# One decode step of attention and a feed-forward layer on one core: a weight transfer cut at row 126, two transfers joined, and one head's softmax put ahead of a loop

## The chip, the cores and the metric

The kernel runs on one NeuronCore of a Trainium2 chip. The core has a matrix engine (TensorE, PE in the profile; PEld is its loading of weights), a vector engine (VectorE, DVE), an activation engine (ScalarE, ACT), GpSimd (POOL) and SyncE (SP), which issues nearly all DMA transfers here. 16 DMA engines move the bytes. TensorE writes only into PSUM; all else lies in SBUF, 128 rows (partitions) wide.

The metric is the device time of one execution in microseconds (us), as the median of several runs. A profiled execution has a time of its own, and a span: from its first to its last profiled instruction.

## The reference

One token of width 512 goes through a modulated attention block with a cache of 32768 positions (32 query heads in 8 groups, a group's four heads share K and V of width 128) and then a modulated feed-forward block.

```python
mod = (_silu(c) @ w_mod).reshape(c.shape[0], 6, 1, -1)
sa, ca, ga, sb, cb, gb = ...
h = _layernorm(x) * (1 + ca) + sa
q = (h @ wq), k and v: the caches, each repeated for 4 query heads
p = _softmax(q @ k^T * 128 ** -0.5)
x = x + ga * ((p @ v) @ wo)
h = _layernorm(x) * (1 + cb) + sb
x = x + gb * (maximum(h @ w1, 0) @ w2)
```

K and V are 8 x 32768 x 128 in bf16, 64 MB each; with wq, wo (4 MB each), w_mod (3 MB), w1 and w2 (1.75 MB each) about 149 MB are read once.

## The kernel before

**The stream.** All large inputs come in one fixed order through one queue (SP): w_mod, wq, then for each group of heads ("head" below, 0 to 7) two tiles of K and two of V of 4 MB each, the K of head h + 1 alternating with the V of head h. The last head's second V tile comes as two halves, then wo in four parts (`WOP`, L47: heads 0 to 3, heads 4 and 5, head 6, head 7), w1 in two pieces, w2 in six (`W2P`, L51). The list is `stream` (L139 to L144); `need` (L147) issues it up to the entry that is asked for, through `load` (L96) and `stream_dma` (L131). Tiles lie in a ring of five slots of 4 MB; a transfer can't start before the slot is free. wo's four parts share one slot and w1 and w2 another. Each transfer takes one of eight completion semaphores in turn, and SP waits, before it issues a transfer, until the earlier one with that semaphore has landed.

**One head.** `turn_k` (L398) transposes a quarter of a K tile in place on VectorE (128 x 2048 as f32), four times per 4 MB tile; `scores` (L412) multiplies each of these with the queries on TensorE, 8 matmuls of 128 x 512; after a tile's 32 matmuls `bank_max` (L427) copies the scores to SBUF and takes their maximum. `softmax` (L433) is a generator, whose steps the schedule places one by one with `next(soft)`: m_p, the maximum of each row (L437); mT, its transpose on TensorE (L440); Mrow and Mexp on VectorE (L443, L448); Mb on TensorE, then nbias and the exponential on ScalarE (L454 to L459); PT, the transposed probabilities, and Lexp on VectorE (L465, L468); L_ps, the sums, on TensorE (L471); and Linv, their reciprocals, on VectorE (L474). `pv` (L477) multiplies PT with a V tile: 32 matmuls, in a hardware loop of 8 turns except in the last tiles, where they are written out. `blocks` (L509) picks Y from the result on VectorE, `o_cols` (L520) turns it on TensorE, `normalise` (L528) divides by the sums, `spread` (L544) shapes a part of wo's heads for `project` (L555), which multiplies them with that part of wo.

**The order.** On TensorE and VectorE the order is the one written in the schedule (L599 on): within each engine, instructions start in that order. In iteration g (L611) head h = g + 1 gets its scores, head g its `pv`, and head g - 1 its `blocks` to `normalise`. The first K tile's four transposes and scores come before the first `pv` loop of g, the second tile's between the first and second loop. Head h's softmax begins at the end of iteration g: its first step before the second `pv` loop of g, the second right behind it, and the rest between the scores of iteration g + 1:

```python
            bank_max(h, 1)
            soft = softmax(h)
            next(soft)
            if g < LOOPED:
                pv(g, (2, 3))
                next(soft)
                continue
```

**The tail.** After the scores of head 7 come `pv` for head 6's second and head 7's V tiles, `project(0)` to `project(3)`, the second layernorm (L691 on), w1 (L714), the relu (L725), w2 (L735), the last two VectorE operations (L740, L742) and the 1 KB output. `keep_clock` (L592) multiplies something whose result is not used, in places where TensorE would else wait. `join_rows` (L576) gathers what the first two parts of wo gave.

Of the kernel before, what the change touches and what calls it, by code (L numbers as in the profile page):

```python
# [17 lines left out]
def kernel(  # L18
# [15 lines left out]
    P = 128  # L34
    _, _, D = A_x.shape
    _, Hkv, Sk, Dh = A_k_cache.shape
    Hq = A_wq.shape[1] // Dh
    REP = Hq // Hkv
# [8 lines left out]
    WOP = [(0, Hkv // 2), (Hkv // 2, Hkv // 4), (Hkv - 2, 1), (Hkv - 1, 1)]  # L47
    WOROWS = 2
    LAST = Hkv - 1
    LOOPED = Hkv - 2  # L50
    W2P = [(0, 4), (4, 7), (7, 10), (10, 12), (12, 13), (13, 14)]  # L51
    W1P = [(0, KT - 1), (KT - 1, KT)]
    assert Dh == 128 and REP == 4 and D == 512 and FT == W2P[-1][1] and NTILE == 4
    scale = float(Dh) ** -0.5
    eps = 1e-5
# [5 lines left out]
    vv = A_v_cache[0].rearrange("g (p j) d -> g p j d", p=P)  # L61
    wm_v = w_mod.rearrange("(p kt) n -> p kt n", p=P)
    wq_v = A_wq.rearrange("(p kt) n -> p kt n", p=P)
    def wo_v(i):
        g0, n = WOP[i]
        return A_wo[g0 * REP * Dh:(g0 + n) * REP * Dh, :].rearrange("(p r) d -> p r d", p=P)

    w1_v = B_w1.rearrange("(p kt) f -> p kt f", p=P)
    w2_v = B_w2.rearrange("(p f) d -> p f d", p=P)

# [15 lines left out]
    loaded, last_loop = {}, []  # L86
# [3 lines left out]
    def piece(name, at, n):  # L90

        if name not in pieces:
            pieces[name] = ring.tile([P, 2 * TK * Dh], BF16, tag="slot", name=name)
        return pieces[name][:, at:at + n]

    def load(key):  # L96
        kind = key[0]
        if kind == "wm":
            t = ring.tile([P, KT, 6 * D], BF16, tag="slot", name="wm_sb")
            src = wm_v  # L100
        elif kind == "wq":
            t = ring.tile([P, KT, Hq * Dh], BF16, tag="slot", name="wq_sb")
            src = wq_v
        elif kind in "kv":
            g, steps = key[1], key[2]
            src = (kv if kind == "k" else vv)[g, :, TK * steps[0]:TK * (steps[-1] + 1), :]
            name = "Ksb" if kind == "k" else "Vsb"
            if len(steps) == 2:
                t = ring.tile([P, TK * len(steps), Dh], BF16, tag="slot", name=name)
            else:  # L110
                t = piece(name, TK * Dh * (steps[0] % 2), TK * Dh).rearrange("p (j d) -> p j d", d=Dh)
        elif kind == "wo":
            g0, n = WOP[key[1]]
            t = piece("wo_sb", g0 * REP * D, n * REP * D).rearrange("p (r d) -> p r d", d=D)
            src = wo_v(key[1])
        elif kind == "w1":
            k0, k1 = W1P[key[1]]
            t = piece("w12_sb", k0 * Dff, (k1 - k0) * Dff).rearrange("p (kt f) -> p kt f", f=Dff)
            src = w1_v[:, k0:k1]
        else:  # L120
            f0, f1 = W2P[key[1]]
            t = piece("w12_sb", KT * Dff + f0 * D, (f1 - f0) * D).rearrange("p (f d) -> p f d", d=D)
            src = w2_v[:, f0:f1]
        stream_dma(t[:], src)
        if kind in "kv":
            for i, u in enumerate(steps):
                loaded[(kind, g, u)] = t[:, TK * i:TK * (i + 1), :]
        else:
            loaded[key] = t[:]

    def stream_dma(dst, src):  # L131
        i = nc.sync.dma_start(out=dst, in_=src)
        tc.stamp_issue_order_token(i.ins, "sp_stream")
        if last_loop:

            tc.add_manual_dep(i.ins, last_loop[0], mybir.DependencyInfo(
                mybir.DependencyClass.NoSync, mybir.DependencyReason.DATA))

    stream = [("wm",), ("wq",)] + [("k", 0, (2 * G, 2 * G + 1)) for G in range(NG)]  # L139
    for g in range(LAST):  # L140
        for G in range(NG):
            stream += [(kind, gg, (2 * G, 2 * G + 1)) for kind, gg in (("k", g + 1), ("v", g))]
    stream += [("v", LAST, (0, 1)), ("v", LAST, (2,)), ("v", LAST, (3,))] + [("wo", i) for i in range(len(WOP))]
    stream += [("w1", i) for i in range(len(W1P))] + [("w2", i) for i in range(len(W2P))]  # L144
    pos = [0]

    def need(key):  # L147
        while key not in loaded:
            load(stream[pos[0]])
            pos[0] += 1  # L150
        return loaded[key]
# [17 lines left out]
    for hp in range(4):  # L169
        h, par = hp // 2, hp % 2  # L170
        src = AP(ib.tensor, ib.offset + 64 * h + par, [[ib.ap[0][0], P], [0, 4], [2, 32]])
# [68 lines left out]
    def bank(name):  # L240
        return ps_s.tile([P, 512], F32, tag="s", name=name)[:]
# [137 lines left out]
    def build_qbd(g):  # L379
        d_ap = qbd[g % 2][:]  # L380
        d_ps = d_ap.ap[0][0]
        s_ap = qrep_sb[:]
        s_ps = s_ap.ap[0][0]
        for a in range(4):
            o = AP(d_ap.tensor, d_ap.offset + (32 * a) * d_ps + 4 * 7 + 32 * a,
                   [[d_ps, 32], [QW, 4], [1, 4]])
            i = AP(s_ap.tensor, s_ap.offset + (32 * a) * s_ps + REP * g,
                   [[s_ps, 32], [Hq, 4], [1, 4]])
            nc.scalar.copy(out=o, in_=i)  # L389
# [8 lines left out]
    def turn_k(g, u, half):  # L398

        if u == 0 and half == 0:  # L400
            S_tiles[g] = spool.tile([P, NG, 512], F32, tag="S_g", name="S_g")
            m_tiles[g] = spool.tile([P, NG], F32, tag="m2", name="m2")
        Ksb = need(("k", g, u))
        KTt = Ksb[:, 32 * half:32 * half + 32, :].rearrange("p j d -> p (j d)")
        t = nc.vector.transpose(out=KTt.bitcast(F32), in_=KTt.bitcast(F32))  # L405
        KT_tiles[g, u, half] = KTt
        if loop:

            tc.add_manual_dep(t.ins, loop.pop(), mybir.DependencyInfo(
                mybir.DependencyClass.NoSync, mybir.DependencyReason.DATA))  # L410

    def scores(g, u, half):  # L412

        t4 = (2 * u + half) % 4
        if t4 == 0:
            S_ps_tiles[g] = bank("S_ps")
        KTv = KT_tiles.pop((g, u, half)).rearrange("p (jj h i par) -> p jj h i par", jj=32, h=2, i=32, par=2)
        for sl in range(2):
            s = 2 * t4 + sl
            for hp in range(4):  # L420
                h, par = hp // 2, hp % 2
                nc.tensor.matmul(  # L422
                    S_ps_tiles[g], lhsT=qbd[g % 2][:, hp, 4 * (7 - s):4 * (7 - s) + P], rhs=KTv[:, 16 * sl:16 * sl + 16, h, :, par],
                    start=(t4 == 0 and sl == 0 and hp == 0), stop=(t4 == 3 and sl == 1 and hp == 3),
                )
# [77 lines left out]
    def open_o(g):  # L503
        o_tiles[g] = ps_o.tile([16, 4 * Dh], F32, tag="o", name="o_ps")
        nc.vector.memset(o_tiles[g][:], 0.0)  # L505
# [93 lines left out]
    with tc.manual_schedule(engines={mybir.EngineType.PE, mybir.EngineType.DVE}):  # L599
# [7 lines left out]
        soft = softmax(0)  # L607
        for _ in soft:
            pass
        soft = None  # L610
        for g in range(LAST):  # L611
            h = g + 1
            build_qbd(h)
            turn_k(h, 0, 0)
            turn_k(h, 0, 1)
            turn_k(h, 1, 0)
            scores(h, 0, 0)
            if soft:
                next(soft)
            open_o(g)  # L620
            scores(h, 0, 1)
            if soft:
                next(soft)
            if g > 0:
                blocks(g - 1)
            scores(h, 1, 0)
            if g > 0:
                o_cols(g - 1)
            turn_k(h, 1, 1)
            scores(h, 1, 1)  # L630
            if soft:
                next(soft)
            if g > 0:
                normalise(g - 1)
                if g in [sum(w) for w in WOP]:
                    spread(part_of(g - 1))
            if soft:
                next(soft)
            bank_max(h, 0)
            next(soft or iter(()), None)  # L640
            pv(g, (0, 1))
            for u in (2, 3):
                for half in range(2):
                    turn_k(h, u, half)
                    scores(h, u, half)
            bank_max(h, 1)
            soft = softmax(h)
            next(soft)
            if g < LOOPED:
                pv(g, (2, 3))  # L650
                next(soft)
# [3 lines that stand above are left out]
            pv(g, (2,), range(6))  # L655
            next(soft)
            next(soft)
            open_o(LAST)
            pv(g, (2,), range(6, 16))
            pv(g, (3,))  # L660
            next(soft)
            next(soft, None)
            a_rows.append(row_bank("a_ps"))
            blocks(g)
# [44 lines left out]
        NQ = 32 * FT  # L709
        for part, (k0, k1) in enumerate(W1P):  # L710
            w1_sb = need(("w1", part))
# [62 lines left out]
```

## Time and profile before

| | |
|---|---|
| time, median of 3 runs | 355.38 us (355.25 to 355.55) |
| time of the profiled execution | 355.74 us |
| its span | 353.9 us, mean granted TensorE clock 0.947 |
| TensorE busy | 279.8 us (79%) |
| VectorE busy | 203.1 us (57%) |
| ScalarE busy | 25.4 us (7%) |
| share of the 16 DMA engines in SP's queue | 98.4% |
| read from HBM | 149.42 MB, 422 GB/s over the span |
| a 4 MB tile, from issue to landing | about 35 us (median) |

The busy time of an engine is an average over stages with different limits. The issue-to-landing time of a tile is mostly time in the queue, since a 4 MB tile alone takes about 9.7 us at this rate. "Granted clock" is the share of full speed at which TensorE was allowed to run; the profile shows stretches at 1.0 and at 0.5. In lists of instructions the idle time before a group and what ended it stand in square brackets.

### The profile page before, as it was taken

Reading aid. Unit: us, or ns where it says so; the run is one execution under the profiler, and the core shown is the slowest. Engines: PE = TensorE matmul, PEld = TensorE weight load, DVE = VectorE, ACT = ScalarE, POOL = GpSimd, SP = SyncE. Lnnn points to the kernel's source line nnn. Section 1 sums busy time; section 2 is a strip of 40 time slices with the busy share of each in tenths; the row PEclk is TensorE's granted clock in tenths of the full one; section 3 lists DMA queues with packets and bytes.
Section 4 is the critical chain, followed back from the end, with each engine's and each line's share of the span. In section 5 each row is a group of like instructions: output and inputs, shape, how many; then the busy total and the mean of one; then the engine's idle time right before and its main releaser. Section 6 shows DMA issues by size and latency. Waiting matters only on the chain. (4 is left out here: it accounts for less than half of the span.)

```text
span 353.9 us, 4006 instructions
## 1 busy us (share of the span) xinstructions
PE 279.8 (79%) x1311; PEld 112.7 (32%) x1311; DVE 203.1 (57%) x271; ACT 25.4 (7%) x69; POOL 3.9 (1%) x16
## 2 busy tenths in 40 slices
PE   0542781999898979897979796979689687989996
PEld 0221230333343323332323232323234233334444
DVE  6245775882768268462939178553938095734142
ACT  1220003000010001000100001000100010002000
POOL 4000000000000000000000000000000000000000
PEclk9995997799899999998999899999999997999999
DMA  8999999999999999999999999999999999999994
GB/s 309 455 422 445 431 422 441 441 418 424 459 418 422 459 418 424 441 437 426 433 444 417 430 456 419 427 446 426 422 448 430 422 439 441 422 430 424 421 420 177
DMA packets 6852, 149.59 MB, mean 423 GB/s; under 512 B 824, under 2 KB 1080, under 8 KB 1976
## 3 DMA queue, kind: packets, MB, share of 16 engines
q1 hardware_dynamic: 6776, 149.43, 98.4%
q8 instruction: 8, 0.13, 0.1%
q14 instruction: 4, 0.03, 0.0%
q0 software_dynamic: 64, 0.00, 0.0%
HBM read 149.42 MB, written 0.00 MB: 422 GB/s over the span
## 5 line engine op out<-in xcount | busy, mean ns | idle before, releaser
L405 DVE STREAM_TRANSPOSE Ksb<-Ksb 128x2048 f32<-128x2048 f32 x64 | 142.9, 2281 | 63.9 <-DMA Ksb<-in_A_k_cache_dram 63.9
L484 PE MATMUL o_ps<-Vsb,PT_g 128*16 (+1 forms) x512 | 130.0, 395 | 21.5 <-ACT qbd L389 7.2
L422 PE MATMUL S_ps<-Ksb,qbd 128*128 128x512 bf16 x512 | 121.8, 388 | 23.5 <-DVE Ksb L405 21.9
L422 PEld LDWEIGHTS <-qbd 128*128 128x128 bf16 x512 | 49.0, 98 | 87.6 <-issue 31.8
L484 PEld LDWEIGHTS o_ps<-Vsb,PT_g 128*16 x416 | 37.4, 90 | 90.2 <-issue 63.7
L428 DVE TENSOR_SCALAR_CACHE_REDUCE S_g<-S_ps 128x512 f32<-128x512 f32 x16 | 11.0, 690 | 34.4 <-PE S_ps L422 34.4
L389 ACT COPY qbd<-qrep_sb 32x16 bf16<-32x16 bf16 x32 | 6.4, 201 | 138.7 <-PE S_ps L422 137.6
L465 DVE STREAM_TRANSPOSE PT_g<-P_g 128x1024 bf16<-128x1024 bf16 x8 | 9.7, 1218 | 6.6 <-ACT P_g L459 6.6
L484 PEld LDWEIGHTS <-PT_g 128*16 128x16 bf16 x96 | 8.2, 90 | 11.0
L456 ACT ACTIVATE nbias<-Mb_ps 128x1 f32<-128x1 f32 x8 | 1.4, 171 | 136.8 <-PE Mb_ps L454 136.8
L459 ACT ACTIVATE P_g<-S_g,nbias 128x1024 bf16<-128x1024 f32 x8 | 9.2, 1148 | 0.2
L227 PE MATMUL xc_ps<-cx_sel,cx_bd 16*128 16x2 bf16 x4 | 0.3, 172 | 11.1 <-DVE cx_bd L221 11.1
L515 DVE SCALAR_TENSOR_TENSOR Y<-o_ps,smask,Y 16x128 f32<-16x128 f32 x24 | 8.1, 339 | 0.8
L471 PE MATMUL L_ps<-Lexp,ones_f 128*128 128x4 f32 x16 | 3.0, 257 | 4.3 <-DVE Lexp L468 4.3
L597 PE MATMUL spare_ps<-qbd,ident_bf 128*128 128x512 bf16 x19 | 5.6, 380 | 0.0
L440 PE MATMUL mT_ps<-ident_f,m_p 128*1 128x128 f32 x8 | 2.2, 270 | 3.9 <-DVE m_p L437 2.0
L471 PEld LDWEIGHTS L_ps<-Lexp,ones_f 128*128 128x128 f32 x16 | 3.1, 221 | 5.8 <-issue 5.1
L443 DVE TENSOR_REDUCE Mrow<-mT_ps 1x4 f32<-1x128 f32 x8 | 2.1, 257 | 4.6 <-PE mT_ps L440 4.6
L534 DVE TENSOR_TENSOR oT_sb<-acc_ps,Linv 128x4 bf16<-128x4 f32 x8 | 1.2, 150 | 5.7 <-PE acc_ps L521 5.7
L295 PE MATMUL mod_ps<-wm_sb,siluT 128*1 128x512 bf16 x24 | 3.6, 624 | 1.0 <-DVE siluT L289 1.0
L505 DVE MEMSET o_ps<- 16x512 f32 x8 | 3.9, 485 | 0.8
L552 DVE CAST o_sb<-o_ps 128x4 bf16<-128x4 f32 (+2 forms) x4 | 0.7, 167 | 5.7 <-PE o_ps L548 5.7
(115 smaller groups left out, 80.0 us busy)
## 6 DMA issues: line engine op xcount, KB each, us to landing
Ksb<-in_A_k_cache_dram SPq DMA_DIRECT2D x16, 4096.0 KB, 35.6
Vsb<-in_A_v_cache_dram SPq DMA_DIRECT2D x15, 4096.0 KB, 35.2
wq_sb<-in_A_wq_dram SPq DMA_DIRECT2D x1, 4096.0 KB, 19.6
Vsb<-in_A_v_cache_dram SPq DMA_DIRECT2D x2, 2048.0 KB, 31.8
wm_sb<-in_w_mod_dram SPq DMA_DIRECT2D x1, 3072.0 KB, 10.4
wo_sb<-in_A_wo_dram SPq DMA_DIRECT2D x1, 2048.0 KB, 29.1
w_sb<-in_B_w_dram SPq DMA_DIRECT2D x1, 1344.0 KB
wo_sb<-in_A_wo_dram SPq DMA_DIRECT2D x1, 1024.0 KB, 31.1
```

The source lines that it names most:

```text
L295: nc.tensor.matmul(dst[j // 4][32 * (j % 4):32 * (j % 4) + 1, :], lhsT=src_T[:, kt:kt + 1], rhs=w[:, kt, j * 512:(j + 1) * 512], start=(kt ...
L389: nc.scalar.copy(out=o, in_=i)
L405: t = nc.vector.transpose(out=KTt.bitcast(F32), in_=KTt.bitcast(F32))
L422: nc.tensor.matmul(S_ps_tiles[g], lhsT=qbd[g % 2][:, hp, 4 * (7 - s):4 * (7 - s) + P], rhs=KTv[:, 16 * sl:16 * sl + 16, h, :, par], start= ...
L428: nc.vector.tensor_scalar(out=S_tiles[g][:, G, :], in0=S_ps_tiles[g], scalar1=1.0, scalar2=None, op0=ALU.mult, op1=ALU.max, accum_out=m_ti ...
L459: nc.scalar.activation(out=P_g[:], in_=S_g[:].rearrange("p g f -> p (g f)"), func=ACT.Exp, bias=nbias[:], scale=scale, accum_out=l_g[:],)
L465: nc.vector.transpose(out=PT_g[:], in_=P_g[:])
L471: nc.tensor.matmul(L_ps[:], lhsT=ones_f[:], rhs=Lexp[:], start=True, stop=True)
L484: nc.tensor.matmul(o_tiles[g][:], lhsT=PT, rhs=Vx, start=False, stop=False, skip_group_check=True)
L505: nc.vector.memset(o_tiles[g][:], 0.0)
L515: nc.vector.scalar_tensor_tensor(out=Y[:], in0=o[:, s], scalar=smask[:, s:s + 1], in1=Y[:], op0=ALU.mult, op1=ALU.add,)
L597: nc.tensor.matmul(spare[0], lhsT=ident_bf[:], rhs=qbd[0][:, :, 0:P], start=True, stop=True)
```

## The change

Three things, in one diff:

- `load` can cut a transfer by rows. w2's second piece (3 of 14 columns, 384 KB) goes as one transfer of rows 0 to 125 and one of rows 126 and 127, both into the same place as before.
- wo's third and fourth part, 512 KB each, are one transfer of 1 MB. A key of the stream now names a tuple of parts; `project(2)` and `project(3)` use their halves of it.
- In iteration g = 5 the softmax of head 6 takes four more steps (mT; Mrow and Mexp; Mb, nbias and the exponential; PT and Lexp) before the second `pv` loop of head 5, and L_ps right behind it. In iteration g = 6 (`ahead`) the fourth K transpose of head 7's first tile comes next to the other three, Linv next, then the four groups of scores with only `open_o` and `blocks` between them, and then `o_cols` and `normalise` of head 5.

The number of transfers is the same. The arithmetic is the same.

```diff
+    EVEN, EVEN_ROWS = ("w2", 1), 126
...
         elif kind == "wo":
-            g0, n = WOP[key[1]]
-            t = piece("wo_sb", g0 * REP * D, n * REP * D).rearrange("p (r d) -> p r d", d=D)
-            src = wo_v(key[1])
+            parts = key[1]
+            (g0, n), m = WOP[parts[0]], len(parts)
+            t = piece("wo_sb", g0 * REP * D, m * n * REP * D).rearrange("p (g x) -> p g x", g=m)
+            src = A_wo[g0 * REP * Dh:(g0 + m * n) * REP * Dh, :].rearrange("(g p r) d -> p g (r d)", g=m, p=P)
...
-        stream_dma(t[:], src)
+        cuts = [0, EVEN_ROWS, P] if key == EVEN else [0, P]
+        for a, b in zip(cuts, cuts[1:]):
+            stream_dma(t[a:b], src[a:b])
...
+        elif kind == "wo":
+            for m, i in enumerate(parts):
+                loaded[("wo", i)] = t[:, m].rearrange("p (r d) -> p r d", d=D)
...
-    stream += [("v", LAST, (0, 1)), ("v", LAST, (2,)), ("v", LAST, (3,))] + [("wo", i) for i in range(len(WOP))]
+    stream += [("v", LAST, (0, 1)), ("v", LAST, (2,)), ("v", LAST, (3,))] + [("wo", parts) for parts in ((0,), (1,), (2, 3))]
...
         for g in range(LAST):
             h = g + 1
+            ahead = h == LAST
             build_qbd(h)
             turn_k(h, 0, 0)
             turn_k(h, 0, 1)
             turn_k(h, 1, 0)
+            if ahead:
+                turn_k(h, 1, 1)
+                next(soft, None)
+                soft = None
             scores(h, 0, 0)
...
             scores(h, 1, 0)
+            if ahead:
+                scores(h, 1, 1)
             if g > 0:
                 o_cols(g - 1)
-            turn_k(h, 1, 1)
-            scores(h, 1, 1)
+            if not ahead:
+                turn_k(h, 1, 1)
+                scores(h, 1, 1)
...
             soft = softmax(h)
             next(soft)
+            if g == LOOPED - 1:
+                for _ in range(4):
+                    next(soft)
             if g < LOOPED:
                 pv(g, (2, 3))
                 next(soft)
```

More of the change, by code (lines that the diff above doesn't have):

```diff
@@ L63 @@
     wq_v = A_wq.rearrange("(p kt) n -> p kt n", p=P)
-    def wo_v(i):
-        g0, n = WOP[i]
-        return A_wo[g0 * REP * Dh:(g0 + n) * REP * Dh, :].rearrange("(p r) d -> p r d", p=P)
     w1_v = B_w1.rearrange("(p kt) f -> p kt f", p=P)
```

## The prediction

> **What bounds the kernel now.** I read the page first (is anything full?), then the chain that ended last, then the timeline of its stages, then the single DMA issues, and last the windows around the stages that looked odd.
>
> ```profile
> DMA  8999999999999999999999999999999999999994
> ```
>
> The DMA engines are full to the last slice, and the page's queue row gives 98.4% of the span to the one queue that SP feeds. The order of the stream therefore fixes when each weight can be there. But the end is made by an engine:
>
> ```profile
> 307.78 7.12 PE S_ps L422 x32
> ...
> 341.80 0.51 PE acc_ps L567 x16
> ...
> 343.25 0.50 PE acc_ps L567 x16
> ...
> 347.89 3.30 PE ffn_ps L735 x56
> ```
>
> The chain of waits (start, us, what) shows TensorE working almost without a gap from 307.8 to 351.2. The two x16 groups are `project(2)` and `project(3)` (L567), x56 is the second matrix of the feed-forward part. The timeline (start, us, engine, line) shows where this chain came from and when the steps of interest begin:
>
> ```profile
> 283.51 6.70 DVE L405 STREAM_TRANSPOSE Ksb<-Ksb 128x2048 f32<-128x2048 f32 x3 [7.53 <-DMA Ksb<-in_A_k_cache_dram]
> ...
> 292.44 2.29 DVE L405 STREAM_TRANSPOSE Ksb<-Ksb 128x2048 f32<-128x2048 f32 x1
> 294.66 1.19 DVE L465 STREAM_TRANSPOSE PT_g<-P_g 128x1024 bf16<-128x1024 bf16 x1
> ...
> 298.65 8.94 PE L484 MATMUL o_ps<-Vsb,PT_g 128*16 x32 [0.66 <-PE L_ps L471]
> ...
> 308.61 0.42 SPq L132 DMA_DIRECT2D wo_sb<-in_A_wo_dram  x1
> ...
> 309.08 0.43 SPq L132 DMA_DIRECT2D wo_sb<-in_A_wo_dram  x1
> ...
> 341.42 0.80 PEld L567 LDWEIGHTS <-wo_sb 128*128 128x128 bf16 x16
> ...
> 341.81 0.33 SPq L132 DMA_DIRECT2D w_sb<-in_B_w_dram  x1
> ```
>
> Between the third and fourth K transpose of head 7 VectorE does head 6's softmax and head 5's Y (290.13 to 292.44), and the loop at 298.65 takes 8.94 us where its sister at 259.48 takes 8.05. The issues, asked one by one, give issue-to-landing times:
>
> ```profile
> wo_sb<-in_A_wo_dram SPq DMA_DIRECT2D x1, 512.0 KB, 31.9
> ...
> wo_sb<-in_A_wo_dram SPq DMA_DIRECT2D x1, 512.0 KB, 32.7
> ...
> w_sb<-in_B_w_dram SPq DMA_DIRECT2D x1, 128.0 KB, 8.7
> ```
>
> So wo's third part lands at 308.61 + 31.9 = 340.5, its fourth at 309.08 + 32.7 = 341.8, w2's last piece at 341.81 + 8.7 = 350.5. The same sum gives w1's second piece 346.05, w2's pieces 347.3, 348.3, 349.3, 349.9, 350.2, 350.5. TensorE uses w2's pieces at 347.89 plus 16, 28, 40, 48, 52 matmuls of 59 ns (3.30 / 56): 348.83, 349.54, 350.25, 350.7, 350.96. The transfers are thus only 0.3 to 0.6 us ahead of the chain.
>
> ```profile
> 292.20:295.60 3.40, 1.67 (x9) 0.81 (x8) 3.40 (x3) 0.17 (x2) 0.00 (x0) 1.00 0.91 395
> 295.60:302.50 6.90, 6.24 (x18) 2.44 (x17) 1.52 (x8) 0.00 (x0) 0.00 (x0) 0.51 0.99 427
> ...
> 348.00:349.00 1.00, 1.00 (x20) 1.00 (x19) 0.00 (x0) 0.08 (x1) 0.00 (x0) 1.00 0.74 275
> 349.00:350.00 1.00, 1.00 (x22) 1.00 (x19) 0.00 (x0) 0.00 (x0) 0.00 (x0) 1.00 0.32 111
> 350.00:351.00 1.00, 1.00 (x22) 0.99 (x18) 0.00 (x0) 0.00 (x0) 0.00 (x0) 1.00 0.01 5
> ```
>
> In the windows (length, busy time of PE, PEld, DVE, ACT, POOL, granted clock, DMA share, GB/s) a stretch with TensorE half idle is followed by one at half clock. And the DMA engines don't finish together: 0.74, 0.32 and 0.01 of them are busy in the three us from 348. Their mean end is 348 + 1.07 = 349.07, the last one's near 350.24, some 1.2 us later.
>
> **Part 1, head 6's softmax ahead.** It removes nothing; it moves mT, Mrow, Mexp, Mb, the exponential, PT and Lexp (L437 to L468) ahead of head 5's second V loop. Mrow, Mexp, PT, Lexp then run on VectorE in its 7.53 us wait for K; no DMA is issued by the moved steps. Cost: TensorE waits for the chain. From the end of m_p (275.97): mT 0.27, Mrow 0.23 to 0.28, Mexp 0.21, Mb 0.22 and some 0.15 of hand-overs make 1.1 us, so the loop starts at 277.8 to 278.0, not 276.87, and ends near 287.4, not 286.28. The next slot's V issue on SP follows it (286.45), with two whole 4 MB transfers still queued: nothing.
> Gain: the four K turns run 283.51 to 292.4 (4 x 2.23). After L_ps, TensorE does 24 scores (7.12 / 32 = 0.22 each) to 293.1 and the last 8 to 294.9; Y, `o_cols`, `normalise`, `spread` follow, and the loop starts near 296.6, 2.0 us earlier. With TensorE denser, no half clock: 8.05 not 8.94, so the loop ends at 304.7, not 307.59. There the gain is cut: head 7's second K tile lands only at 302.99, VectorE turns it until 311.88, and the last 8 scores need 1.8: 313.7 against 314.90. Bounds: 0 to -1.2 at the end of the scores; taken -1.2, so TensorE could be at `project(2)` at 340.2. wo's earlier parts (landed 336.9, 339.2) allow that.
>
> **Part 2, wo's two last parts as one.** SP issues one transfer fewer (0.43 us on a queue that then waits anyway). Its 1 MB is in place when the fourth part was: 341.8. `project(2)` now waits for all of it, where it had been ready at 340.5; behind it on TensorE stand `join_rows`, `project(3)` and all that follows. From landing to use the trace has 0.05 to 0.1: the K tile issued at 267.74 lands 35.2 later, at 302.94, and VectorE starts at 302.99; wq, 1.2 + 19.6 = 20.8, and TensorE at 20.89. So `project(2)` starts at 341.9 against 341.42: **+0.49**. TensorE is busy for 3.00 of 3.00 us from 341.4 to 344.4, so nothing takes this up again, and part 1's -1.2 is lost in that wait. Bounds: 0 if the transfer lands 0.5 earlier, +0.5 as traced.
>
> **Part 3, w2's second piece as 126 rows and 2.** The count of transfers stays the same. Each takes one of eight semaphores in turn and waits for the one that had it before (w2's pieces were issued at 336.86, 339.27, 340.52 and 341.81, each as a part of wo landed); w2's last now follows w1's first piece instead of wo's last: about 345 (three quarters of w1's bytes, between 341.8 and 346.05) instead of 341.8. Its landing is due at 350.5, and out's own issue to the end of the span is 2.06 (351.84 to 353.9), so it isn't late. The trace has no transfer of 126 rows. A 384 KB piece follows its neighbour by 1.0 us, 16 engines sharing it. If the last engine is spared its share, later pieces gain up to the 0.95 to 1.0; if only half the engines carry it, they lose as much. I take 0, since with part 2 w2 is needed 0.49 later and has 0.8 to 1.0 us in hand; the bad end costs 1.0 - 0.8 = 0.2.
> [...]
>
> **Sum.** Against the profiled execution, 355.74 (span 353.9 and 1.84 around it): -1.2 that is lost, +0.49, 0: 356.23. The shown runs have a median 0.36 lower, 355.38. Either that is a constant, and then 355.87; or ordinary runs lack the half-clock stage, come 1.1 us earlier to the tail, and are held by w2's landings 0.3 later, which is just 355.4; part 2's hold doesn't move with the clock, so 356.23 stands. The second reading explains the 0.36, so I lean to it: **356.1** (own range 355.7 to 356.5).
>
> **Rivals.**
> 1. *The last DMA engine isn't late in ordinary runs* (not slower). For: 0.01 of DMA share after 350, one engine alone, so its lag decides each landing. Against: the page counts 12 packets of instructions on these engines, which any run needs, and a lag they make would be in all. With wo landing with the mean engine, 1.2 earlier, `project(2)` starts at 340.7: 0.7 before today's. 355.74 - 0.7 = 355.0, less up to 0.36: 354.7. It decides once the landing is 0.85 (0.49 + 0.36) earlier.
> 2. *The clock falls in the tail.* TensorE idles from 340.4 to 341.9 for wo. Half-idle stretches (1.67 of 3.40) were followed by half clock; 1.58 of 3.40 at 275.2 was not. Here 1.9 of 3.4 stays busy, over both. It decides below 1.7; then `project` to ffn runs at half clock for 3.4 us, +1.7: 357.9.
> [...]
> 3. *126 rows land late*: +0.49 and 0.2: 356.4, as priced in part 3.
>
> **Chances.** Forecast 0.60, rival 1 0.27, rival 2 0.08, rival 3 0.05. A measurement of this kernel tells 0.2% (0.7 us) from no change: the line is 356.09 upward, 354.67 downward. The forecast lies across it: 0.36 slower, 0.24 same. Rival 1: 0.12 faster, 0.15 same. Rivals 2 and 3: 0.13 slower. Together slower 0.49, same 0.39, faster 0.12. Range 354.9 to 356.9: beyond it lie rival 2 and the lower end of rival 1.
>
> **What would show it.** Right: the weight load of `project(2)` waits on wo's DMA, at about 341.9; the loop over head 6's first V starts near 296.6; the four K turns are adjacent; the scores of head 7 end near 313.7; no half clock at 295 to 302. Wrong: `project(2)` begins before 341.4 (rival 1), a granted clock under 0.6 after 340 (rival 2), a wait of ffn on w2 (rival 3), or a last landing of w2 before 349.9, which would tell that the split spares the engine that decides.

## The result, and the profile after

The changed kernel takes 356.68 us (median of 6 runs, 356.42 to 357.05); the kernel before, beside it, 355.25 (6 runs, 355.06 to 355.55). The ratio is 1.0039, with a 95% interval of 1.0029 to 1.0049: slower by 1.4 us. The profiled execution takes 357.05 us (before 355.74), its span is 355.3 (before 353.9).

The chain of waits of the changed kernel (start, us, what) no longer ends in TensorE alone. A DMA into w2's tile stands in front of the last 40 matmuls:

```profile
326.95 23.15 DMA w_sb<-in_B_w_dram
350.10 0.04 issue
350.14 2.41 PE ffn_ps L749 x40
352.55 0.02 issue
```

Its timeline (start, us, engine, line, operands; idle time before and what ended it in brackets) at the places that the prediction named:

```profile
283.37 8.89 DVE L408 STREAM_TRANSPOSE Ksb<-Ksb 128x2048 f32<-128x2048 f32 x4 [3.43 <-DMA Ksb<-in_A_k_cache_dram]
...
297.84 8.96 PE L487 MATMUL o_ps<-Vsb,PT_g 128*16 x32 [1.58 <-DVE S_g L431]
...
336.75 0.38 PE L564 MATMUL a_ps<-wo_sb,o_sb 128*1 128x512 bf16 x3
...
341.65 0.69 PE L570 MATMUL acc_ps<-o_sb,wo_sb 128*128 128x1 bf16 x16 [0.60 <-DMA wo_sb<-in_A_wo_dram]
...
346.13 0.93 PE L728 MATMUL hid_ps<-w_sb,h2T 128*1 128x448 bf16 x16
...
348.57 1.05 PE L749 MATMUL ffn_ps<-w_sb,hid_bd 128*4 128x128 bf16 x16 [0.76 <-DMA w_sb<-in_B_w_dram]
350.14 2.39 PE L749 MATMUL ffn_ps<-w_sb,hid_bd 128*4 128x128 bf16 x40 [0.52 <-DMA w_sb<-in_B_w_dram]
```

The same steps in the kernel before:

```profile
337.42 0.38 PE L561 MATMUL a_ps<-wo_sb,o_sb 128*1 128x512 bf16 x3
...
341.63 0.67 PE L567 MATMUL acc_ps<-o_sb,wo_sb 128*128 128x1 bf16 x16
...
346.09 0.93 PE L714 MATMUL hid_ps<-w_sb,h2T 128*1 128x448 bf16 x16
...
347.89 3.29 PE L735 MATMUL ffn_ps<-w_sb,hid_bd 128*4 128x128 bf16 x56
```

The four K turns are adjacent, and `project(2)` waits for wo, both as predicted. But `hid` (w1, L728) starts at 346.13, where it started at 346.09 before: up to there nothing is lost. The loss is behind it. The 56 matmuls of ffn, one unbroken group of 3.29 us before, now stand in two groups, with 0.76 and 0.52 us of waiting for w2 in front of them. ffn thus starts 0.68 us later (348.57 against 347.89), and the second wait adds 0.52: 1.20 of the 1.36 us by which it ends later (352.55 against 351.19).

The windows say why w2 is late. Columns: stretch, its length, busy time (count) of PE, PEld, DVE, ACT, POOL, granted clock, DMA share, GB/s. First the kernel before, then the changed one:

```profile
346.00:347.00 1.00, 1.00 (x18) 0.35 (x18) 0.22 (x2) 0.00 (x0) 0.00 (x0) 1.00 0.99 386
347.00:348.00 1.00, 0.88 (x9) 0.26 (x6) 0.71 (x2) 0.42 (x2) 0.00 (x0) 1.00 1.04 404
```

```profile
345.00:346.00 1.00, 1.00 (x6) 0.20 (x4) 0.70 (x6) 0.29 (x1) 0.00 (x0) 1.00 1.13 356
346.00:347.00 1.00, 1.00 (x18) 0.30 (x17) 0.27 (x2) 0.00 (x0) 0.00 (x0) 1.00 1.00 247
347.00:348.00 1.00, 0.81 (x7) 0.20 (x3) 0.71 (x2) 0.38 (x2) 0.00 (x0) 1.00 1.04 236
348.00:349.00 1.00, 0.43 (x8) 0.46 (x9) 0.00 (x0) 0.12 (x1) 0.00 (x0) 1.00 0.99 225
349.00:350.00 1.00, 0.62 (x12) 0.49 (x9) 0.00 (x0) 0.00 (x0) 0.00 (x0) 1.00 0.91 290
```

Read the last two columns together. The DMA engines are as busy as before (share about 1), yet they move 225 to 247 GB/s where they moved 386 to 404. They aren't idle, and a share of about 1 is all 16 of them: each packet takes longer. The single packets that the trace records say so directly. A packet carries one row of a piece, so its size tells whose it is. Packets of 4096 bytes, from w2's first piece, take a median of 159 ns in the kernel before and of 258 ns from 346 to 347 in the changed one. Packets of 3072 bytes, from the two 384 KB pieces, take a median of 121 ns before, and 188, 207 and 218 ns in the three us from 346. The slow stretch starts before 346, so it also holds the last of w1 and w2's first piece, which were not cut.

### The profile page after: what moved, and what is told of

The parts are those of the page before. It is cut to its first block, busy times and chain, and to the rows that moved or that the text cites. A ratio compares the mean times of both kernels' runs of the same rounds, so it can differ in the third digit from the quotient of the medians.

```text
span 355.3 us, 4007 instructions
## 1 busy us (share of the span) xinstructions
PE 279.4 (79%) x1311; PEld 112.2 (32%) x1311; DVE 203.4 (57%) x271; ACT 25.4 (7%) x69; POOL 3.9 (1%) x16
## 5 line engine op out<-in xcount | busy, mean ns | idle before, releaser
L749 PE MATMUL ffn_ps<-w_sb,hid_bd 128*4 128x128 bf16 x56 | 3.4, 219 | 1.3 <-DMA w_sb<-in_B_w_dram 1.3
```

The costliest lines, as they stand in the source:

```text
L749: nc.tensor.matmul(ffn_ps, lhsT=hid_bd[:, ft, i, :], rhs=w2_sb[:, ft - f0, i * P:(i + 1) * P], start=(ft == 0 and i == 0), stop=(ft == FT ...
```

## The experiments

All of them compute the whole of the reference. Each time is a median, each ratio is to the kernel before on the same chip, with its 95% interval.

**Is it the cut by rows?** Four kernels: the changed one without the cut; with the piece cut by columns in its place, which keeps the number of transfers; with the cut at row 112; and the kernel before with only the cut.

```diff
# e1_whole
-        cuts = [0, EVEN_ROWS, P] if key == EVEN else [0, P]
+        cuts = [0, P]
# e2_columns
+        cuts = [0, 2, 3] if key == EVEN else [None, None]
...
+            stream_dma(t[:, a:b], src[:, a:b])
# e3_112
+    EVEN, EVEN_ROWS = ("w2", 1), 112
# e4_cut_alone (in the kernel before)
-        stream_dma(t[:], src)
+        cuts = [0, 126, P] if key == ("w2", 1) else [0, P]
+        for a, b in zip(cuts, cuts[1:]):
+            stream_dma(t[a:b], src[a:b])
```

> The changed kernel with w2's second piece as one transfer of 128 rows again (parts 1 and 2 alone). Theory A (while rows 0 to 125 are moved the DMA engines stay busy but move about half as much: 236 and 225 GB/s at a share near 1.0 in the windows from 347 to 349 of the changed kernel, against 404 and 275 before, where the work ran out in 348 to 349): the whole loss of 1.4 us goes, the time is within 0.3 us of the kernel before, project(2) still waits for wo until about 341.6. Theory B (the loss is wo's wait, as the prediction's sum had it): at least 0.5 us slower than before, 355.7 or more. [...]

> The changed kernel with w2's second piece cut by columns (2 and 1 of its 3 columns, all 128 rows in both) instead of by rows: the same number of transfers, the same semaphores in turn, w2's last still issued after w1's first piece, at about 344.9. Theory A: like the run with the piece whole, within 0.3 us of the kernel before. Theory D (one more transfer, or the late issue of w2's last, leaves a gap): as slow as the changed kernel, 356.4 to 357.

> The changed kernel with the cut at row 112 (112 and 16 rows). If it is the uneven spread over engines that costs (126 rows don't divide by 16, 112 do), the rate holds at about 400 GB/s and the time is within 0.4 us of the kernel before. If a transfer that doesn't fill all 128 rows is what runs slowly, whichever engines carry it, it is as slow as the changed kernel: 356.3 or more, with windows of about half the rate at full share.

> The kernel before with nothing but w2's second piece cut at row 126 (part 3 alone, one transfer more). Theory A: slower than before by 1.3 to 1.8 us, 356.6 to 357, with w2's later pieces landing 1 to 2 us later than the 348.3 to 350.5 before. Theory B: no slower than 0.3 us. [...]

| | us | runs | ratio to before |
|---|---|---|---|
| e1_whole | 356.17 (355.76 to 357.05) | 8 | 1.0027 (1.0017 to 1.0038) |
| e2_columns | 355.69 (355.44 to 356.27) | 11 | 1.0008 (0.9999 to 1.0017) |
| e3_112 | 356.53 (356.21 to 356.81) | 8 | 1.0029 (1.0019 to 1.0039) |
| e4_cut_alone | 357.26 (356.85 to 358.51) | 6 | 1.0062 (1.0046 to 1.0078) |

The cut by columns has as many transfers as the changed kernel and the same order, and takes 1.0 us less. In its windows the engines keep their rate, and its ffn is unbroken again:

```profile
346.00:347.00 1.00, 1.00 (x18) 0.31 (x18) 0.26 (x2) 0.00 (x0) 0.00 (x0) 1.00 1.00 370
347.00:348.00 1.00, 0.88 (x9) 0.26 (x6) 0.71 (x2) 0.39 (x2) 0.00 (x0) 1.00 1.05 403
```

```profile
347.93 3.29 PE L749 MATMUL ffn_ps<-w_sb,hid_bd 128*4 128x128 bf16 x56
```

So neither one transfer more nor a later issue is the cause; which rows a transfer holds is. The cut at 112 is as slow as the one at 126 (356.53 against 356.68), although 112 and 16 can be divided by 16, the page's count of DMA engines, and 126 and 2 can't: that isn't it. And the cut alone, in the old order, costs 1.9 us (1.6 to 2.8 by its interval): it needs neither of the other parts. That it should cost more alone than in the changed kernel isn't shown: two of its six runs lie near 358.5, and its profiled execution, at 356.96, is as fast as the changed kernel's, at 357.05. Two things didn't fit. e1_whole was expected much nearer to the kernel before than +0.8; its interval overlaps the changed kernel's (1.0029 to 1.0049), so it wouldn't show the cause by itself. And it came out slower than e2_columns, from which it differs by one column cut. No run has the large part of a row cut without the small one.

**Which part costs the rest?** Each of the other two parts alone: e5_softmax_alone has the new order with the stream of the kernel before, e6_wo_alone the joined wo with the old order.

```diff
# e5_softmax_alone (in the changed kernel)
-        cuts = [0, EVEN_ROWS, P] if key == EVEN else [0, P]
+        cuts = [0, P]
...
-    stream += ... [("wo", parts) for parts in ((0,), (1,), (2, 3))]
+    stream += ... [("wo", parts) for parts in ((0,), (1,), (2,), (3,))]
# e6_wo_alone (in the changed kernel)
-        cuts = [0, EVEN_ROWS, P] if key == EVEN else [0, P]
+        cuts = [0, P]
...
-            ahead = h == LAST
+            ahead = False
...
-            if g == LOOPED - 1:
+            if False:
```

> Head 6's softmax ahead alone (part 1): the order of the changed kernel, the stream of the kernel before. The run without the row cut (parts 1 and 2) was 356.17, the kernel before beside it 355.39. Theory H: part 1 costs by itself, since TensorE waits longer (275.3 to 278.7 busy 0.23, and 296 to 298) and what follows runs at half clock: 355.8 to 356.3, and half clock shows at 278 to 282 and at 299 to 304 in the windows. Theory W: part 2's wait for the joined wo costs the 0.3 to 0.8, part 1 is lost in it: then without it 354.7 to 355.4, and the weight load of project(2) does not wait on a DMA.

> wo's two last parts as one transfer alone (part 2): the order of the kernel before, w2 whole. Theory W (the wait for the joined wo costs what it shifts project(2) by, at most 0.5): 355.7 to 355.9, with project(2) at 341.6 to 341.9 behind a DMA. Theory H (the cost lies in part 1): within 0.2 of the kernel before, 355.2 to 355.6, with hid at most 0.1 later.

The softmax alone: 355.62 (355.14 to 356.58, 11 runs), ratio 1.0005 (0.9996 to 1.0014), no difference that can be told; it lies between the ranges of the two theories. The joined wo alone: 355.74 (355.54 to 356.15, 11 runs), ratio 1.001 (1.0001 to 1.0019), some 0.3 us, as the theory of wo's wait had it.

**How does the price of a row cut grow?** e7_wo0_126 leaves w2 whole and cuts wo's first part, 2 MB, at row 126; e8_twice cuts both 384 KB pieces of w2.

```diff
# e7_wo0_126
-    EVEN, EVEN_ROWS = ("w2", 1), 126
+    EVEN, EVEN_ROWS = ("wo", (0,)), 126
# e8_twice
+        cuts = [0, EVEN_ROWS, P] if key in (EVEN, ("w2", 2)) else [0, P]
```

> The changed kernel with the cut at row 126 moved from w2's second piece (384 KB) to wo's first part (2 MB); w2's pieces are whole. Theory P (the price grows with the bytes: a transfer of fewer than 128 rows moves at about 230 GB/s, not 420, while the DMA share stays near 1): the part takes about 9 us, not 5, lands near 341, and project(0) and all behind it come about 4 us later: 359.5 to 360.5. Theory F (a fixed price for each cut transfer, 1.5 to 1.9 us as the cut of w2 showed alone): 357.0 to 358.0. [...]

> The changed kernel with both 384 KB pieces of w2 (the second and the third) cut at row 126. The changed kernel was 356.68. Theory P (half rate for the bytes of a cut piece): the third piece loses another 0.8 to 1.0 us, the last landing of w2 goes from 352.0 to about 353, time 357.4 to 357.8. Theory S (the first cut sets off a disturbance of the queue that the pieces behind it share anyway): within 0.3 of the changed kernel, 356.5 to 357.0.

The 2 MB cut: 363.54 us (362.83 to 363.64, 4 runs), ratio 1.022 (1.0205 to 1.0236). Two cuts in w2: 358.04 (357.99 to 358.17, 4 runs), ratio 1.0071 (1.0056 to 1.0087), 1.36 above the changed kernel and 0.24 above the upper end of what was expected of a price by bytes. The windows of e7_wo0_126, and the weight load that waits for that part:

```profile
334.00:336.00 2.00, 2.00 (x11) 0.87 (x10) 0.41 (x1) 0.00 (x0) 0.00 (x0) 1.00 1.09 246
336.00:338.00 2.00, 1.17 (x6) 0.29 (x4) 0.72 (x3) 0.00 (x0) 0.00 (x0) 1.00 1.03 233
338.00:340.00 2.00, 0.00 (x0) 0.00 (x0) 0.63 (x2) 0.00 (x0) 0.00 (x0) 0.80 0.98 195
340.00:342.00 2.00, 0.00 (x0) 0.00 (x0) 0.00 (x0) 0.00 (x0) 0.00 (x0) 0.50 0.94 174
```

```profile
342.88 0.08 PEld L564 LDWEIGHTS <-o_sb 128*1 128x1 bf16 x1 [6.21 <-DMA wo_sb<-in_A_wo_dram]
```

The low rate lasts from about 332 to 342, again at a DMA share near 1, and `project(0)` starts some 6 us later than in the changed kernel. wo's second part, which wasn't cut, is slowed with it: its packets of 8192 bytes take medians of 561 to 659 ns between 332 and 342, and 309 in the changed kernel. The price thus grows with the bytes of the cut transfer, here nearly all in the 126 rows, since the other two hold 32 KB; the rate is lower than the 230 GB/s that the expectation took, and TensorE, idle for 6 us, had a granted clock of 0.50 from 340 to 348, and of 0.64 on the mean from 348 to 350. Both put the time above the expected 360.5. In e8_twice ffn waits a third time, in front of the third piece:

```profile
348.32 1.05 PE L749 MATMUL ffn_ps<-w_sb,hid_bd 128*4 128x128 bf16 x16 [0.63 <-DMA w_sb<-in_B_w_dram]
349.95 0.83 PE L749 MATMUL ffn_ps<-w_sb,hid_bd 128*4 128x128 bf16 x12 [0.58 <-DMA w_sb<-in_B_w_dram]
351.43 1.72 PE L749 MATMUL ffn_ps<-w_sb,hid_bd 128*4 128x128 bf16 x28 [0.65 <-DMA w_sb<-in_B_w_dram]
```

**Does the row of the cut matter?** e9_120 cuts at row 120. e10_filled is e1_whole with multiplications in TensorE's waits, whose result isn't used, against half clock; e11_whole_again is e1_whole once more; e12_finer is part 1 alone with those multiplications and smaller last pieces of w2, meant to beat both kernels.

```diff
# e9_120
+    EVEN, EVEN_ROWS = ("w2", 1), 120
# e10_filled, e12_finer (both also with cuts = [0, P])
+            if ahead:
+                fill_ps = bank("fill_ps")
+                fill(fill_ps, 1)
...
+            if ahead:
+                fill(fill_ps, 4)
...
+                fill_ps = bank("fill_ps")
+                for n in (3, 0, 2, 0):
+                    fill(fill_ps, n)
                     next(soft)
+                fill(fill_ps, 3)
# e12_finer (also with wo in four parts again)
-    W2P = [(0, 4), (4, 7), (7, 10), (10, 12), (12, 13), (13, 14)]
+    W2P = [(0, 4), (4, 7), (7, 9), (9, 11), (11, 13), (13, 14)]
```

> The changed kernel with the cut at row 120 (120 rows and 8) in place of 126 and 2. Theory A (any transfer that does not cover all 128 rows moves at about half rate, w2's landings 1.0 to 1.5 us late): 356.4 to 356.9, like the cuts at 126 (356.68) and at 112 (356.53), and the chain of waits ends in a DMA into w_sb. [...]

> Parts 1 and 2 without the row cut (it was 356.17), with 8 multiplications of 128x512 whose result is not used in TensorE's waits before the second V loop of head 5, and 5 in those before the first V loop of head 6. Theory H (the clock: half-busy stretches before these loops bring half clock in them, up to 0.9 us each, in some runs on the later one): no half clock at 278 to 284 and at 299 to 304, the tail waits for wo at 341.6, all runs below 356.1, median 355.6 to 355.8. Theory Q (the clock is not it; the w2 stream or the joined wo makes the 0.8): 356.0 to 356.4, and runs near 357 stay.

> Parts 1 and 2 without the row cut once more, on the chip of the filled one, since its first 8 runs lay in two groups (355.8 to 356.2 and 356.9 to 357.05). Theory H: 355.7 to 356.2 again, with some runs near 357, and slower than the filled one by 0.2 to 0.6. If the first result was the luck of 8 runs: 355.6 to 355.8, like the cut by columns (355.69).

> A version meant to beat both: part 1 alone (355.62) with the same filling multiplications, wo in four parts, and w2's last pieces as 2, 2, 2, 1 columns in place of 3, 2, 1, 1. In the run of part 1 alone ffn waited for the third piece of w2 to 349.34, with 28 matmuls (1.74) behind it. If that wait sets the end, the third piece lands a third of a us earlier and the span shortens by 0.2 to 0.4: 355.0 to 355.3. If the last landing sets it (350.5, then 4 matmuls), nothing is gained: 355.4 to 355.6.

| | us | runs | ratio to before |
|---|---|---|---|
| e9_120 | 356.68 (356.56 to 357.17) | 4 | 1.0040 (1.0025 to 1.0054) |
| e10_filled | 357.00 (356.05 to 357.12) | 5 | 1.0046 (1.0034 to 1.0059) |
| e11_whole_again | 355.83 (355.47 to 357.08) | 10 | 1.0019 (1.0008 to 1.0029) |
| e12_finer | 355.43 (355.21 to 356.01) | 11 | 1.0004 (0.9995 to 1.0013) |

120 rows are as slow as 126 and 112. The row isn't it: each of the three cuts, which leave some of the 128 rows to a second transfer, has the low rate. A window of e3_112 and one of e9_120:

```profile
347.00:348.00 1.00, 0.92 (x7) 0.21 (x3) 0.71 (x2) 0.27 (x2) 0.00 (x0) 1.00 1.06 250
```

```profile
347.00:348.00 1.00, 0.66 (x3) 0.10 (x1) 0.67 (x2) 0.50 (x2) 0.00 (x0) 1.00 1.02 231
```

The filling missed. Its profile shows a granted clock of 1.00 from 270 to 305, where e1_whole had two stretches at half clock, yet four of its five runs lie near 357 (the profiled one is the fifth, 356.05). One of the four, at 357.02, has the same mean granted clock as the profiled one, 0.952. So more half clock isn't needed for a run near 357, and half clock in these two loops is unlikely to be what makes such runs of e1_whole. Its two sets of runs together have a median of 356.1, with 5 of 18 near 357; e2_columns has none of 11 above 356.27. None of the runs near 357 was profiled, so what makes them stays open. Between the profiled executions of e1_whole and e2_columns (356.23 and 355.76) half clock does make a difference: head 6's first V loop takes 8.97 us in the one (granted clock 0.50 from 301 to 303) and 8.12 in the other (1.00), and `project(2)` starts at 342.07 and 341.64.

e10_filled and e12_finer have the same order and the same filling from here to `project(0)`, and so show something else. The timeline of head 6's last scores, the loop over head 6's first V and `project(0)`, first of e12_finer, then of e10_filled:

```profile
267.53 7.32 PE L425 MATMUL S_ps<-Ksb,qbd 128*128 128x512 bf16 x32 [0.19 <-PEq L493]
...
298.37 8.05 PE L487 MATMUL o_ps<-Vsb,PT_g 128*16 x32 [0.69 <-PE fill_ps L597]
...
336.70 0.38 PE L564 MATMUL a_ps<-wo_sb,o_sb 128*1 128x512 bf16 x3
```

```profile
269.07 7.12 PE L425 MATMUL S_ps<-Ksb,qbd 128*128 128x512 bf16 x32 [0.19 <-PEq L493]
...
299.63 8.05 PE L487 MATMUL o_ps<-Vsb,PT_g 128*16 x32 [0.69 <-PE fill_ps L597]
...
337.67 0.38 PE L564 MATMUL a_ps<-wo_sb,o_sb 128*1 128x512 bf16 x3
```

e10_filled comes 1.54 us late to these scores, and 1.26 and 0.97 of that are still there at the loop and at `project(0)`. With the old order it is otherwise. The profiles of the kernel before and of e6_wo_alone differ by 1.30 at the same scores:

```profile
267.76 7.29 PE L422 MATMUL S_ps<-Ksb,qbd 128*128 128x512 bf16 x32 [0.23 <-PEq L490]
...
292.67 0.38 PE L521 MATMUL acc_ps<-mask_sb,Y 16*128 16x4 f32 x2
294.78 2.77 PE L422 MATMUL S_ps<-Ksb,qbd 128*128 128x512 bf16 x8 [1.73 <-DVE Ksb L405]
```

```profile
269.06 7.12 PE L425 MATMUL S_ps<-Ksb,qbd 128*128 128x512 bf16 x32 [0.19 <-PEq L493]
...
293.18 0.38 PE L524 MATMUL acc_ps<-mask_sb,Y 16*128 16x4 f32 x2
294.55 1.90 PE L425 MATMUL S_ps<-Ksb,qbd 128*128 128x512 bf16 x8 [0.98 <-DVE Ksb L408]
...
336.65 1.15 PE L564 MATMUL a_ps<-wo_sb,o_sb 128*1 128x512 bf16 x16
```

1.30 have become 0.51 at head 5's Y, and nothing at the next scores, since TensorE waits there for VectorE's fourth turn of K. Three profiles without half clock in the later loop say the same. From the same scores at 269.06 and 269.05 the old order comes to `project(0)` at 336.65 (e6_wo_alone), the new one at 337.33 (e9_120), and the new one from 267.48 at 336.63 (e8_twice). The wait that part 1 removes was also a place where lateness was taken up, as far as these few profiles can show it.

e12_finer is level with the kernel before. Its ffn starts at 347.24, 0.65 earlier than before's 347.89, but is stopped by w2 until 350.03 and ends at 350.87, 0.33 earlier in the profile. The two kernels can't be told apart, and no version here beats the kernel before.

## Why the prediction was right and where it wasn't

It said 356.1, slower or level, and 356.68 lies in its range of 354.9 to 356.9 but above the likeliest case's own 355.7 to 356.5. The side is right and the sum is not: its terms were mis-sized, and the one taken as nothing is the largest. That the number still came within 0.6 is partly luck, since the errors have opposite signs. Of the signs named beforehand, one for being wrong appeared: ffn waits for w2, which stood for rival 3.

*Part 3, taken as 0 with a bad end of 0.2: this step failed.* The same transfers with a column cut take 1.0 us less (by their ratios 1.1; against e1_whole and its repetition 0.4 and 0.7), and the row cut alone adds 1.9 to the kernel before. Rival 3 named the mechanism, w2 landing late and ffn waiting for it, with a chance of 0.05 and a price a fifth or less of what it costs. The price was bounded by the piece's own bytes: 1.0 us late at most, of which 0.8 were in hand. Three things were wrong. What runs beside the cut piece is slowed too (packets of 258 ns from 346 to 347, where they took 159), so w2's first piece, which wasn't cut, is late (ffn waits for it to 348.57, where all was ready at 347.89 before); only 0.59 was in hand there. The 0.8 counted on part 2 to delay ffn by 0.49, and without the row cut part 2 moves it by 0.04 (347.93 in e2_columns). And the cut piece follows it 1.57 us later (348.57 to 350.14), not 1.0, which makes the second wait.

No run shows what makes the packets of a row cut slow, nor how many engines carry the cut piece, on which the prediction's gain and loss for this part rested. What the runs show is the rate: 225 to 256 GB/s between 346 and 349 in the changed kernel and in e9_120, and 174 to 246 between 332 and 342 in e7_wo0_126, against 386 and 404 from 346 to 348 in the kernel before.

*Part 2, +0.49.* `project(2)` does wait for wo, as forecast, but to 341.65 instead of 341.9, and its matmuls began at 341.63 before. The prediction took the start of the weight load, 341.42, for that of the matmuls; before, these first let two filling matmuls end. So 0.02 is lost there and 0.04 at `hid`, in this profile. Over runs the part costs 0.3 (0.04 to 0.7, from its ratio). That it costs more over runs than in this profile fits the prediction's second reading of the 0.36: in e4_cut_alone, with the old order, wo in four parts and no half clock in the later loop, `project(2)` starts at 340.49, 1.1 earlier than in the profile before, and in e6_wo_alone, as early up to there, it waits 1.05 for the joined wo.

*Part 1, -1.2 lost in the wait.* The later start of head 5's loop (278.40, forecast 277.8 to 278.0) and the adjacent K turns are there. The loop over head 6's first V starts at 297.84, 1.2 later than forecast; its row names a wait of 1.58 for VectorE's copy of the scores (S_g), which the sum left out. And the half clock that was to vanish didn't, as the windows of the changed kernel show:

```profile
275.30:278.70 3.40, 0.78 (x4) 0.38 (x4) 1.09 (x6) 1.41 (x3) 0.00 (x0) 1.00 0.96 414
278.70:282.10 3.40, 3.40 (x10) 1.11 (x9) 1.24 (x2) 0.00 (x0) 0.00 (x0) 0.50 0.98 424
295.80:299.20 3.40, 1.52 (x7) 0.61 (x7) 0.99 (x4) 0.00 (x0) 0.00 (x0) 1.00 0.94 405
299.20:302.60 3.40, 3.40 (x10) 1.15 (x9) 0.00 (x0) 0.00 (x0) 0.00 (x0) 0.50 1.01 434
```

Two stretches in which TensorE is idle for half the time or more are each followed by one at half clock. The earlier of them is part 1's own: TensorE now waits for head 6's softmax chain there, and pays for the clock in head 5's loop. The scores of head 7 end at 314.15, not 313.7, and `project(0)` comes 0.67 earlier than before (336.75 against 337.42), not 1.2. Even that isn't the order's doing: without half clock in the later loop, e6_wo_alone with the old order comes to it at 336.65 and e8_twice with the new one at 336.63. In both, the last scores of head 7 wait for VectorE's turn of K (to 311.70 and 311.68), the limit that the prediction named. The net effect of part 1 is nothing that can be told, alone (1.0005), as forecast, though its gain is absent rather than lost in the wait.

*Rivals 1 and 2.* The joined wo lands as late as forecast to within 0.3, so rival 1 is out in this profile; in ordinary runs, for which it was meant, the joined wo alone comes out 0.3 slower, not faster. The granted clock after 340 is 1.00, so rival 2 is out.

## What to carry to other kernels

A piece of a weight that must come earlier or in parts was better cut along its columns than along its rows here: three row cuts of 384 KB cost about the same whatever the row (356.53 to 356.68 us), the cost grew with the bytes (363.54 us with 2 MB cut), and one column cut cost nothing that could be told (355.69, ratio 1.0008). When a transfer's shape is new to a trace, bound its price by what it may do to its neighbours in the queue as well as by its own bytes. And a wait on an engine that others overtake is a buffer for lateness from upstream: ask what it takes up before it is removed.

## What the runs showed of the hardware that was not expected

- DMA engines can be busy throughout and move little more than half, or less: a share of 0.99 to 1.04 with 225 to 247 GB/s, for some three us with 384 KB cut, and of 0.88 to 1.09 with 174 to 246 GB/s for some ten with 2 MB cut, where the kernel before moves 386 and 404 from 346 to 348. The share alone wouldn't have shown it; the share beside the GB/s does.
- A row cut of a 384 KB piece delayed the piece that was issued before it: ffn waits for that one until 348.57, where the kernel before starts ffn at 347.89 without a wait for w2.
- A stretch of 3.4 us with TensorE half idle was often followed by half clock, but not always. In the changed kernel 0.78 of 3.40 us busy from 275.3 and 1.52 from 295.8 were followed by 3.4 us at 0.50, in the kernel before 1.67 from 292.2 by 6.9 us at 0.51. But there 1.48 from 275.1 was followed by 1.00. Where the stretch is laid also decides what it says. In e9_120 one from 296.9 has 1.30 us busy and is followed by 1.00. But that trace's clock is at 0.50 from 280.7 to 284.1, and counted on from there in steps of the same 3.4 us, the stretch is 297.7 to 301.1, and TensorE is busy for 1.80 of it:

```profile
280.70:284.10 3.40, 3.22 (x9) 1.11 (x9) 1.38 (x3) 0.00 (x0) 0.00 (x0) 0.50 1.05 453
...
297.70:301.10 3.40, 1.80 (x9) 0.68 (x8) 0.77 (x3) 0.00 (x0) 0.00 (x0) 1.00 1.07 463
301.10:304.50 3.40, 3.39 (x15) 1.09 (x13) 1.78 (x1) 0.00 (x0) 0.00 (x0) 1.00 1.03 443
```

  So in these profiles 0.78, 1.52 and 1.67 of 3.4 us busy came before half clock, and 1.48 and 1.80 before full clock.
